# Six kinds of small matmuls with a moving operand of 32 or 64 columns in place of 1 to 32

## The chip, the cores and the metric

The kernel runs on one core of one Trainium2 chip. The metric is the device time of one execution in microseconds, given as the median of several runs.

## The reference

Two layers of a decode step for four tokens (batch B = 4, one query each). A layer is attention over the last 2048 positions of a cache, with a residual, and then a gated feed-forward with a residual. Both layers use the same weights and the same caches.

```python
W = 2048                                  # of 8192 cached positions
q = (layernorm(x) @ wq).reshape(B, 16, 256)            # 16 query heads, 8 kv heads
scores = q . k[:, :, -W:] * 256 ** -0.5                # a kv head serves 2 query heads
o = softmax(scores) . v[:, :, -W:]
x = x + o.reshape(B, 4096) @ wo                        # D = 448
h = layernorm(x)
x = x + (silu(h @ w_gate) * (h @ w_up)) @ w_down       # F = 1792
# ... the same two steps once more
```

## The kernel before

The work is cut into pairs of a token and a kv head: 4 tokens, 2 layers and 8 kv heads make 64 pairs. A written table gathers them into 48 groups of one or two pairs. Each group needs the K and V windows of its pairs, 1 MB each, which SP's queue loads into a pool of 34 buffers of 512 KB. Some of them are kept for the second layer. All engines work through orders that are written out by hand as tables of numbers, one per engine, and a small graph places the semaphore waits between them. A buffer is loaded again only after its last reader is done, so the speed of the engines decides when transfers start.

One group goes through these steps. DVE transposes K in place (L853). PE multiplies K with the query (L886, the scores, tile S). DVE takes the maximum per partition (L902, into `tiny`). PE runs the *spread* (L907 and L910): one matmul writes a mask of large negative numbers, and a second adds the maxima of the partitions that belong to one head, so that DVE can take the maximum over them (L916, `negm`). ACT takes the exponential (L920). PE turns the probabilities (L936, tile Y), ACT copies them to pT (L946), PE sums them (L954), DVE and POOL make the reciprocal (L959, L981). PE multiplies with V (L968). ACT and DVE split the result into even and odd parts (L984, L986, `oh`), PE *flips* it back into columns (L992), DVE scales it into oT (L1026), and PE applies wo, as rows (L1046) or as columns (L1038).

The last group goes without the flip. It multiplies V as the weights with the probabilities as the moving operand (L1006, `vs`), which gives columns at once.

At the end of a token's attention the rows are collected: ACT and DVE write them as a high and a low part (L771, L773), PE *turns* them into columns (L781), and DVE adds the residual (L785). The norm follows (L544 to L570), and the feed-forward, with tokens as columns (L730 gate and up, L758 *down*, L766 the residual) or as rows (L666, L694). The feed-forward of the last token has a version of its own (L1152 to L1217) behind the last projection (L1074, L1083).

Some matmuls repeat their moving operand already: in `ffn` a helper named `more` reads the columns of n tokens over and over until 32 are filled, and only the first n of the result are used. PE's order also holds filler matmuls (L1313) with weights of zero and 512 columns, which add nothing to the tile that they name.

The names of the tiles in the profile are those of the first tensor of a kind: `wide` holds the rows and the feed-forward's middle, `tiny` small constants (among them the maxima, `osel` and `rsel`), `small` small numbers in fp32, `half` the pool of buffers.

Of the kernel before, what the change touches and what calls it, by code (L numbers as in the profile page):

```python
# [351 lines left out]
def build(nc, A_x, A_k_cache, A_v_cache, A_wq, A_wo, B_x, B_w_gate, B_w_up, B_w_down, out):  # L352
# [3 lines left out]
    with ExitStack() as es:  # L356
# [342 lines left out]
        def ffn(ts):  # L699
            n, sl = len(ts), span(ts)  # L700
            gw, rep = NFC * n, 32 // n
            cw = n * rep
            th, hc = wide[:, 0:gw], wideb[:, 256:256 + gw]

            def more(ap):
                return ap.unsqueeze(1).broadcast_to([128, rep, n])

            def block(zb, f):
                return zb[:, cw * f:cw * f + cw].rearrange("p (r t) -> p r t", t=n)

            def once(zb, f):
                return zb[:, 0:cw * f].rearrange("p (f x) -> p f x", x=cw)[:, :, 0:n]
            for t in ts:
                s, k = st[:, t, :], f"st{t}"
                g.op(POOL, "fh", lambda e, s=s: e.tensor_single_scalar(s[:, 11:12], s[:, 8:9], 0.5, op=ALU.mult),
                     r=(k + "r2",), w=(k + "s",))
                g.op(POOL, "ft", lambda e, s=s: e.tensor_scalar(s[:, 14:15], s[:, 8:9], s[:, 11:12], None, op0=ALU.mult),
                     r=(k + "r2", k + "s"), w=(k + "t",))

            def gu(e, gi, c0, c1):  # L720
                last = None
                w = (wg_sb, wu_sb)[gi]
                for cc in range(c0, c1):
                    for fc in range(NFC):
                        if cc < 3:
                            lhsT, rhs = w[:, cc * FF + fc * 128:cc * FF + fc * 128 + 128], xn[:, cc, sl]
                        else:
                            lhsT = w[:, 3 * FF + (fc % 7) * 128:3 * FF + (fc % 7) * 128 + 128]
                            rhs = xe[:, fc // 7, sl]
                        last = e.matmul(block((Zb, Z2)[gi], fc), lhsT=lhsT, rhs=more(rhs),  # L730
                                        start=(fc == 0 and cc == 0), stop=(cc == 3), skip_group_check=True)
                return last
            rn, rx = tuple(f"xn{t}" for t in ts), tuple(f"xe{t}" for t in ts)
            for gi, (z, bank, w) in enumerate((("z", "Z", "wg"), ("z2", "Z2", "wu"))):
                g.op(PE, "guc3", lambda e, gi=gi: gu(e, gi, 0, 3), r=rn + (w + "a",), w=(z,), bank=(bank,))
                g.op(PE, "guc1", lambda e, gi=gi: gu(e, gi, 3, 4), r=rx + (w + "b",), acc=(z,), bank=(bank,))

            def tok(ap, j):
                return ap.rearrange("p (f t) -> p t f", t=n)[:, j, :]
            for j, t in enumerate(ts):  # L740
                g.op(SCA, "tanhc", lambda e, j=j, t=t: e.activation(
                    tok(th, j), once(Zb, NFC)[:, :, j], ACT.Tanh, scale=st[:, t, 11:12]),
                    r=("z", f"st{t}s"), w=("wa",), bank=("Z",))
            vec("fca", lambda e: e.scalar_tensor_tensor(
                out=th.rearrange("p (f t) -> p f t", t=n), in0=th.rearrange("p (f t) -> p f t", t=n), scalar=1.0,
                in1=once(Zb, NFC), op0=ALU.add, op1=ALU.mult), ("z",), ("wa",), ("Z",))
            for j, t in enumerate(ts):
                vec("fcb", lambda e, j=j, t=t: e.scalar_tensor_tensor(
                    out=tok(hc, j), in0=tok(th, j), scalar=st[:, t, 14:15],
                    in1=once(Z2, NFC)[:, :, j], op0=ALU.mult, op1=ALU.mult),  # L750
                    ("wa", "z2", f"st{t}t"), ("wa", "wb"), ("Z2",))

            def down(e):
                k, last = 0, None
                for cc in range(4):
                    c0 = 128 * cc if cc < 3 else D - 128
                    for fc in range(NFC):
                        last = e.matmul(block(Zb, cc), lhsT=wd_sb[:, fc, c0:c0 + 128],  # L758
                                        rhs=more(hc[:, n * fc:n * fc + n]), start=(k == 0), stop=(k == 4 * NFC - 1),
                                        skip_group_check=True)  # L760
                        k += 1
                return last
            g.op(PE, "downc", down, r=WIDE + ("wd",), w=("z",), bank=("Z",))
            for j, t in enumerate(ts):
                for x, key in ((xr, f"x{t}"), (xs, f"xs{t}")):
                    vec("fx", lambda e, j=j, t=t, x=x: e.tensor_tensor(  # L766
                        x[:, t, :], x[:, t, :], once(Zb, 4)[:, :, j],
                        op=ALU.add), ("z", key), (key,), ("Z",))

        def rows(t):  # L770
            g.op(SCA, "rowcp", lambda e: e.activation(wideb[:, 0:D], Ab[:, 0:D], ACT.Copy), r=(f"row{t}",), w=("wa",),  # L771
                 bank=("A",))
            vec("rowsub", lambda e: e.tensor_tensor(wideb[:, 512:512 + D], Ab[:, 0:D], wideb[:, 0:D], op=ALU.subtract),  # L773
                (f"row{t}", "wa"), ("wb",), ("A",))

            def turn(e):
                last = None
                for i in range(2):
                    for cc in range(4):
                        c0 = 512 * i + (128 * cc if cc < 3 else D - 128)  # L780
                        last = e.matmul(Zb[:, cc:cc + 1], lhsT=wideb[:, c0:c0 + 128], rhs=rsel[:, t:t + 1],  # L781
                                        start=(i == 0 and cc == 0), stop=(i == 1), skip_group_check=True)
                return last
            g.op(PE, "rturn", turn, r=WIDE + ("rsel",), w=("z",), bank=("Z",))
            vec("rowadd", lambda e: e.tensor_tensor(xr[:, t, :], xs[:, t, :], Zb[:, 0:4], op=ALU.add), ("z", f"xs{t}"),  # L785
                (f"x{t}",), ("Z",))

        def residual(t):
# [37 lines left out]
        def group(gi, members, outs, split, last=False):  # L826
# [77 lines left out]
                r=(f"s{s_}",), w=(f"pmax{s_}",), bank=(f"S{s_}",))  # L904

            def spread(e):
                e.matmul(Sb[s_][0:R, 256:288], lhsT=identb[0:R, 0:R],  # L907
                         rhs=far[0:R, :, :, :].broadcast_to([R, 2, 8, 2]) if w_ == 2 else
                         far1[0:R, :, :].broadcast_to([R, 16, 2]), start=True, stop=False, skip_group_check=True)
                return e.matmul(  # L910
                    Sb[s_][0:R, 256:288].rearrange("p (q x) -> p q x", x=8),
                    lhsT=pmax[s_][0:R, 0:1].broadcast_to([R, R]),
                    rhs=identb[0:R, :].rearrange("p (q x) -> p q x", q=4)[:, :, 0:8], start=False, stop=True,
                    skip_group_check=True)
            g.op(PE, "spread", spread, r=(f"pmax{s_}", "identb", "far", "far1"), w=(f"m{s_}",), bank=(f"S{s_}",))
            g.op(DVE, "negm", lambda e: e.tensor_reduce(  # L916
                negm[s_][0:R, 0:1], Sb[s_][0:R, 256:288], AX.X, ALU.max, negate=True),
                r=(f"m{s_}",), w=(f"negm{s_}",), bank=(f"S{s_}",))
            def ex(e):
                return e.activation(  # L920
# [68 lines left out]

            def flip(e):  # L990
                for dh in range(2):
                    last = e.matmul(Yb[p_][:, 2 * n * dh:2 * n * dh + 2 * n],  # L992
                                    lhsT=oh[:, :].rearrange("p (m e) -> p e m", e=2)[:, dh, :],
                                    rhs=osel[:, 0:2 * n], start=dh == 0, stop=dh == 1, skip_group_check=True)
                return last
            if not last:
                g.op(PE, "flip", flip, r=("oh", "osel"), w=(f"yp{p_}",), bank=(f"Y{p_}",))
# [1 line left out]
            def vs(e, P, hv):  # L999
                x = None  # L1000
                for a in range(2):
                    for gg in range(4):
                        v = unit(vss[P][hv])[:, 1024 * a + 256 * gg:1024 * a + 256 * gg + 256]
                        for dh in range(2):
                            c0 = 32 * (n * dh + P)
                            x = e.matmul(Yb[p_][:, c0:c0 + 32].rearrange("p (r n) -> p r n", n=2),  # L1006
                                         lhsT=v.rearrange("p (m e) -> p e m", e=2)[:, dh, :],
                                         rhs=(pT[pt][:, gg, 2 * a + hv, 8 * P:8 * P + 2] if n == 2 else
                                              p1[:, gg % 2, 2 * a + gg // 2, hv, 0, :]).unsqueeze(1).broadcast_to(
                                                  [128, 16, 2]),  # L1010
                                         start=P == hv == a == gg == dh == 0, stop=False, skip_group_check=True)
                return x
            for P, (pp, t, layer, kvh) in enumerate(members if last else []):
                for hv in range(2):
# [1 line left out]
                    o = g.op(PE, "vs", lambda e, P=P, hv=hv: vs(e, P, hv), r=(f"pT{pt}", f"v{t}_{kvh}_{hv}"),  # L1016
                             bank=(f"Y{p_}",), **kw)
                    o.rel = (vss[P][hv],)
            yo = Yb[p_][:, 0:4 * n].rearrange("p (d P n) -> p d P n", d=2, n=2)
            if last:  # L1020
                yo = Yb[p_][:, 0:64 * n].rearrange("p (d P x) -> p d P x", d=2, P=n)[:, :, :, 0:2]
            for oi, Ps, ts in outs:
                o_ = oT[oi]
                src = yo[:, :, Ps[0]:Ps[-1] + 1, :]
# [355 lines left out]
```

## Time and profile before

| | |
|---|---|
| median of 3 runs | 288.78 us |
| lowest and highest | 287.57 and 292.31 us |
| the profiled execution | 289.3 us |
| its span, from the first to the last instruction | 287.4 us |
| mean granted clock of TensorE, as a share of full speed | 0.958 |
| PE busy | 226.3 us (79% of the span) |
| DVE busy | 190.1 us (66%) |
| ACT busy | 60.8 us (21%) |
| POOL busy | 82.0 us (29%) |
| moved by DMA | 105.66 MB, mean 368 GB/s |

PE is the matmuls, PEld the loads of weights that go on beside them, DVE, ACT and POOL the other engines, SP the engine whose queue issues the loads. In a row by shape, `Z<-wide,wd_sb 128*128 128x32 bf16 x112` names the output, the inputs, the rows and columns of weights in use, the moving operand as partitions times columns, and how many there were. Matmuls overlap, so the time of one in such a row is longer than its distance from the next.

### The profile page before, as it was taken

Reading aid. Unit: us, or ns where it says so; the run is one execution under the profiler, and the core shown is the slowest. Engines: PE = TensorE matmul, PEld = TensorE weight load, DVE = VectorE, ACT = ScalarE, POOL = GpSimd, SP = SyncE. Lnnn points to the kernel's source line nnn. Section 1 sums busy time; section 2 is a strip of 40 time slices with the busy share of each in tenths; the row PEclk is TensorE's granted clock in tenths of the full one; section 3 lists DMA queues with packets and bytes.
Section 4 is the critical chain, followed back from the end, with each engine's and each line's share of the span. In section 5 each row is a group of like instructions: output and inputs, shape, how many; then the busy total and the mean of one; then the engine's idle time right before and its main releaser. Section 6 shows DMA issues by size and latency. Waiting matters only on the chain.

```text
span 287.4 us, 10703 instructions
## 1 busy us (share of the span) xinstructions
PE 226.3 (79%) x4710; PEld 129.9 (45%) x4710; DVE 190.1 (66%) x586; ACT 60.8 (21%) x173; POOL 82.0 (29%) x228
## 2 busy tenths in 40 slices
PE   5011679978888698697987989989987599988686
PEld 1000224454474444354444654454554347655476
DVE  2598738945512578976954898768689559758532
ACT  2000011312301221122232112222432131224210
POOL 1000241323022313222432142630542325243241
PEclk9999999989999989999999999989999959999959
DMA  7999999999996999999999999999999998799900
GB/s 288 412 419 417 419 411 407 396 404 407 393 380 190 349 414 415 417 405 408 351 388 403 424 415 409 414 412 409 413 413 408 406 368 299 212 386 412 392 16 4
DMA packets 26311, 105.66 MB, mean 368 GB/s; under 512 B 2580, under 2 KB 6680, under 8 KB 21528
## 3 DMA queue, kind: packets, MB, share of 16 engines
q1 hardware_dynamic: 26256, 104.97, 92.5%
q8 instruction: 37, 0.61, 0.8%
q14 instruction: 10, 0.08, 0.1%
q10 hardware_dynamic: 8, 0.00, 0.0%
HBM read 104.96 MB, written 0.00 MB: 365 GB/s over the span
## 4 chain that ended last, share of the span: by engine, by line
PE 45%; DMA 24%; DVE 20%; issue 5%; ACT 3%; SPq 2%; POOL 1%; DVEq 0%; ACTq 0%
DMA half<-in_A_v_cache_dram 15%; DVE half L853 10%; PE S L886 10%; PE Y L968 6%; DMA half<-in_A_k_cache_dram 5%; DMA wo_sb<-in_A_wo_dram 4%; PE Z L1313 4%; PE A L1046 3%; PE Z L730 2%; PE S L1313 2%; PE Y L936 2%; PE Z L604 2%; DVE oh L986 2%; PE Z L550 2%; PE Z L666 2%
## 5 line engine op out<-in xcount | busy, mean ns | idle before, releaser
L853 DVE STREAM_TRANSPOSE half<-half 128x1024 uint32<-128x1024 uint32 x86 | 104.3, 1228 | 6.6 <-DMA half<-in_A_k_cache_dram 6.6
L981 POOL TENSOR_TENSOR small<-small 128x2 f32<-128x2 f32 (+1 forms) x48 | 38.4, 805 | 50.9 <-DVE small L959 46.2
L968 PE MATMUL Y<-half,pT 128*4 128x256 bf16 (+1 forms) x992 | 45.2, 279 | 7.2 <-issue 3.6
L886 PE MATMUL S<-half,qe 128*8 128x128 bf16 (+1 forms) x1536 | 44.9, 244 | 6.4 <-issue 2.4
L886 PEld LDWEIGHTS S<-half,qe 128*8 128x8 bf16 x1536 | 30.2, 86 | 19.3 <-issue 5.2
L1313 PE MATMUL Z<-identb,small 128*128 128x512 bf16 x111 | 36.8, 388 | 0.4 <-DVE wide L627 0.4
L920 ACT ACTIVATE praw<-S,small 104x128 bf16<-104x128 f32 (+1 forms) x48 | 19.3, 401 | 53.0 <-DVE small L916 45.8
L892 POOL TENSOR_TENSOR qe<-qc,tiny 128x64 bf16<-128x64 bf16 x64 | 17.8, 292 | 39.7 <-PE S L886 27.1
L986 DVE SCALAR_TENSOR_TENSOR oh<-oh,small,Y 128x256 bf16<-128x256 bf16 x47 | 22.1, 470 | 8.9 <-ACT oh L984 8.4
L968 PEld LDWEIGHTS Y<-half,pT 128*4 128x4 bf16 (+1 forms) x992 | 19.0, 84 | 18.6 <-issue 6.4
L984 ACT ACTIVATE oh<-Y 128x256 bf16<-128x256 f32 x47 | 18.0, 382 | 44.2 <-PE Y L968 31.6
L902 DVE TENSOR_REDUCE tiny<-S 104x1 bf16<-104x128 f32 (+1 forms) x48 | 15.7, 329 | 10.2 <-PE S L886 9.8
L566 POOL TENSOR_SCALAR st<-st 128x1 f32<-128x1 f32 x15 | 4.0, 264 | 58.0 <-DVE st L556 57.8
L946 ACT ACTIVATE pT<-Y 128x64 bf16<-128x64 f32 (+1 forms) x48 | 12.2, 257 | 36.9 <-PE Y L936 29.4
L1046 PE MATMUL A<-wo_sb,oT 128*4 128x448 bf16 x204 | 17.8, 384 | 1.3 <-DVE oT L1026 1.2
L1313 PE MATMUL A<-identb,small 128*128 128x512 bf16 x38 | 15.8, 496 | 2.9 <-DVE A L444 2.7
L1247 POOL MEMSET oT<- 128x16 bf16 x37 | 4.0, 111 | 45.6 <-PE A L1046 31.9
L610 ACT ACTIVATE wide<-Z,small 128x512 bf16<-128x512 f32 x10 | 6.4, 684 | 48.2 <-PE Z L604 38.5
L550 PE MATMUL Z<-st,small 128*128 128x2 f32 x30 | 6.6, 290 | 12.6 <-DVE selt L461 9.3
L1026 DVE TENSOR_TENSOR oT<-Y,small 128x4 bf16<-128x4 f32 (+1 forms) x63 | 9.0, 156 | 10.4 <-PE Y L992 7.0
L959 DVE TENSOR_REDUCE small<-Y 128x2 f32<-128x32 f32 (+1 forms) x48 | 9.1, 190 | 9.3 <-PE Y L954 8.9
L916 DVE TENSOR_REDUCE small<-S 104x1 f32<-104x32 f32 x48 | 8.4, 176 | 8.0 <-PE S L910 7.7
(188 smaller groups left out, 302.0 us busy)
## 6 DMA issues: line engine op xcount, KB each, us to landing
half<-in_A_v_cache_dram SPq DMA_DIRECT2D x91, 512.0 KB, 9.8
half<-in_A_k_cache_dram SPq DMA_DIRECT2D x34, 1024.0 KB, 9.7
half<-in_A_k_cache_dram SPq DMA_DIRECT2D x18, 512.0 KB, 8.0
wo_sb<-in_A_wo_dram SPq DMA_DIRECT2D x8, 448.0 KB, 11.5
half<-in_A_wq_dram SPq DMA_DIRECT2D x3, 1024.0 KB, 16.3
wd_sb<-in_B_w_down_dram SPq DMA_DIRECT2D x1, 1568.0 KB, 16.7
wg_sb<-in_B_w_gate_dram SPq DMA_DIRECT2D x1, 1344.0 KB, 10.1
wu_sb<-in_B_w_up_dram SPq DMA_DIRECT2D x1, 1344.0 KB, 13.1
```

What stands on the lines that cost most here:

```text
L550: g.op(PE, "nstat", lambda e: e.matmul(Z2[:, 0:2], lhsT=onesf[:, 0:1].broadcast_to([128, 128]), rhs=s[:, 0:2], start=True, stop=True, skip ...
L853: return e.transpose(a, a)
L886: last = e.matmul(Sb[s_][qd:qd + 8, 0:32 * 2 * J], lhsT=qe[q_][:, P, ce, :, :].rearrange("p a n -> p (a n)"), rhs=keys(kcs[P], J * x, J, c ...
L892: g.op(POOL, "qe", lambda e, P=P, t=t, kvh=kvh: e.tensor_tensor(qe[q_][:, P, :, :, :], qc[t][:, kvh, :, :].unsqueeze(2).broadcast_to([128, ...
L902: g.op(DVE, f"max{w_}", lambda e: e.tensor_reduce(pmax[s_][0:R, :], Sb[s_][0:R, 0:N], AX.X, ALU.max), r=(f"s{s_}",), w=(f"pmax{s_}",), ban ...
L920: return e.activation(praw[0:R, 0:N].rearrange("p (g r l) -> p g r l", g=2 * w_, l=2), Sb[s_][0:R, 0:N].rearrange("p (l g r) -> p g r l", ...
L968: last = e.matmul(Yb[p_][32 * gg:32 * gg + M, 256:512], lhsT=pT[pt][:, gg, 2 * a + hv, 4 * P:4 * P + M] if n == 2 else p3[:, gg, 2 * a + h ...
L981: g.op(POOL, f"pow{n}", lambda e: e.tensor_tensor(ri[p_][:, 0:2 * n], rs[p_][:, 0:2 * n], expo[:, 1:1 + 2 * n], op=ALU.pow), r=(f"rs{p_}", ...
L984: g.op(SCA, "oh", lambda e: e.activation(oh[:, :], Yb[p_][:, 256:512], ACT.Copy), r=(f"y{p_}",), w=("oh",), bank=(f"Y{p_}",))
L986: g.op(DVE, "oho", lambda e: e.scalar_tensor_tensor(out=oh[:, :], in0=oh[:, :], scalar=lomask[:, 0:1], in1=Yb[p_][:, 256:512], op0=ALU.mul ...
L1046: last = e.matmul(Ab[32 * k:32 * k + B, 0:D], lhsT=oT[oi][:, k % 2, k // 2, :], rhs=wo_sb[:, 4 * kvh + k, :], start=False, stop=False, ski ...
L1313: return e.matmul(fill_banks[b][:, 0:512], lhsT=zero[:, 0:1].broadcast_to([128, 128]), rhs=identb[:, :].unsqueeze(1).broadcast_to([128, 4, ...
```

## The change

Six kinds of matmuls read their moving operand repeatedly, until it has 32 or 64 columns, and write as many columns of the output. The later reader takes the first copy only, out of columns that lie further apart.

| matmul | lines | count | columns before | columns now |
|---|---|---|---|---|
| down projection, tokens as columns | L758 | 112 | 32 | 64 |
| turn of the rows | L781 | 88 | 1 | 32 |
| spread, the mask | L907 | 48 | 32 | 64 |
| spread, the maxima | L910 | 48 | 32 | 64 |
| flip | L992 | 94 | 2 or 4 | 64 |
| V times probabilities in the last group | L1006 | 64 | 32 | 64 |

The readers are L766, L785, L916 and L1026. On every engine the same instructions stand in the same order as before; PE's differ in these widths only, and the waits, the buffers and the fillers stay.

```diff
             def down(e):
-                        last = e.matmul(block(Zb, cc), lhsT=wd_sb[:, fc, c0:c0 + 128],
-                                        rhs=more(hc[:, n * fc:n * fc + n]), ...
+                        last = e.matmul(Zb[:, 64 * cc:64 * cc + 64].rearrange("p (r t) -> p r t", t=n),
+                                        lhsT=wd_sb[:, fc, c0:c0 + 128],
+                                        rhs=hc[:, n * fc:n * fc + n].unsqueeze(1).broadcast_to([128, 64 // n, n]), ...
             vec("fx", ...
-                        x[:, t, :], x[:, t, :], once(Zb, 4)[:, :, j],
+                        x[:, t, :], x[:, t, :], Zb[:, 0:256].rearrange("p (f x) -> p f x", x=64)[:, :, j],
...
             def turn(e):
-                        last = e.matmul(Zb[:, cc:cc + 1], lhsT=wideb[:, c0:c0 + 128], rhs=rsel[:, t:t + 1],
+                        last = e.matmul(Zb[:, 32 * cc:32 * cc + 32], lhsT=wideb[:, c0:c0 + 128],
+                                        rhs=rsel[:, t:t + 1].broadcast_to([128, 32]),
...
             def spread(e):
-                e.matmul(Sb[s_][0:R, 256:288], lhsT=identb[0:R, 0:R],
-                         rhs=far[0:R, :, :, :].broadcast_to([R, 2, 8, 2]) if w_ == 2 else
-                         far1[0:R, :, :].broadcast_to([R, 16, 2]), ...
+                e.matmul(Sb[s_][0:R, 256:320], lhsT=identb[0:R, 0:R],
+                         rhs=far[0:R, :, :, :].broadcast_to([R, 2, 16, 2]) if w_ == 2 else
+                         far1[0:R, :, :].broadcast_to([R, 32, 2]), ...
                 return e.matmul(
-                    Sb[s_][0:R, 256:288].rearrange("p (q x) -> p q x", x=8),
+                    Sb[s_][0:R, 256:320].rearrange("p (q r x) -> p q r x", r=2, x=8),
                     lhsT=pmax[s_][0:R, 0:1].broadcast_to([R, R]),
-                    rhs=identb[0:R, :].rearrange("p (q x) -> p q x", q=4)[:, :, 0:8], ...
+                    rhs=identb[0:R, :].rearrange("p (q x) -> p q x", q=4)[:, :, 0:8].unsqueeze(2).broadcast_to([R, 4, 2, 8]), ...
             g.op(DVE, "negm", lambda e: e.tensor_reduce(
-                negm[s_][0:R, 0:1], Sb[s_][0:R, 256:288], AX.X, ALU.max, negate=True),
+                negm[s_][0:R, 0:1], Sb[s_][0:R, 256:320].rearrange("p (q r x) -> p q r x", r=2, x=8)[:, :, 0, :], AX.XY, ALU.max, negate=True),
...
             def flip(e):
-                    last = e.matmul(Yb[p_][:, 2 * n * dh:2 * n * dh + 2 * n],
+                    last = e.matmul(Yb[p_][:, 64 * dh:64 * dh + 64].rearrange("p (r x) -> p r x", x=2 * n),
                                     lhsT=oh[:, :].rearrange("p (m e) -> p e m", e=2)[:, dh, :],
-                                    rhs=osel[:, 0:2 * n], ...
+                                    rhs=osel[:, 0:2 * n].unsqueeze(1).broadcast_to([128, 32 // n, 2 * n]),
...
             def vs(e, P, hv):
-                            c0 = 32 * (n * dh + P)
-                            x = e.matmul(Yb[p_][:, c0:c0 + 32].rearrange("p (r n) -> p r n", n=2),
+                            c0 = 64 * (n * dh + P)
+                            x = e.matmul(Yb[p_][:, c0:c0 + 64].rearrange("p (r n) -> p r n", n=2),
-                                                  [128, 16, 2]),
+                                                  [128, 32, 2]),
```

More of the change, by code (lines that the diff above doesn't have):

```diff
@@ L757, in down @@
                     for fc in range(NFC):
-                        last = e.matmul(block(Zb, cc), lhsT=wd_sb[:, fc, c0:c0 + 128],
-                                        rhs=more(hc[:, n * fc:n * fc + n]), start=(k == 0), stop=(k == 4 * NFC - 1),
+                        last = e.matmul(Zb[:, 64 * cc:64 * cc + 64].rearrange("p (r t) -> p r t", t=n),
+                                        lhsT=wd_sb[:, fc, c0:c0 + 128],
+                                        rhs=hc[:, n * fc:n * fc + n].unsqueeze(1).broadcast_to([128, 64 // n, n]), start=(k == 0), stop=(k == 4 * NFC - 1),
                                         skip_group_check=True)
@@ L784, in rows @@
             g.op(PE, "rturn", turn, r=WIDE + ("rsel",), w=("z",), bank=("Z",))
-            vec("rowadd", lambda e: e.tensor_tensor(xr[:, t, :], xs[:, t, :], Zb[:, 0:4], op=ALU.add), ("z", f"xs{t}"),
+            vec("rowadd", lambda e: e.tensor_tensor(
+                xr[:, t, :], xs[:, t, :], Zb[:, 0:128].rearrange("p (c x) -> p c x", x=32)[:, :, 0], op=ALU.add), ("z", f"xs{t}"),
                 (f"x{t}",), ("Z",))
@@ L906, in spread @@
             def spread(e):
-                e.matmul(Sb[s_][0:R, 256:288], lhsT=identb[0:R, 0:R],
-                         rhs=far[0:R, :, :, :].broadcast_to([R, 2, 8, 2]) if w_ == 2 else
-                         far1[0:R, :, :].broadcast_to([R, 16, 2]), start=True, stop=False, skip_group_check=True)
+                e.matmul(Sb[s_][0:R, 256:320], lhsT=identb[0:R, 0:R],
+                         rhs=far[0:R, :, :, :].broadcast_to([R, 2, 16, 2]) if w_ == 2 else
+                         far1[0:R, :, :].broadcast_to([R, 32, 2]), start=True, stop=False, skip_group_check=True)
                 return e.matmul(
-                    Sb[s_][0:R, 256:288].rearrange("p (q x) -> p q x", x=8),
+                    Sb[s_][0:R, 256:320].rearrange("p (q r x) -> p q r x", r=2, x=8),
                     lhsT=pmax[s_][0:R, 0:1].broadcast_to([R, R]),
-                    rhs=identb[0:R, :].rearrange("p (q x) -> p q x", q=4)[:, :, 0:8], start=False, stop=True,
+                    rhs=identb[0:R, :].rearrange("p (q x) -> p q x", q=4)[:, :, 0:8].unsqueeze(2).broadcast_to([R, 4, 2, 8]), start=False, stop=True,
                     skip_group_check=True)
@@ L991, in flip @@
                 for dh in range(2):
-                    last = e.matmul(Yb[p_][:, 2 * n * dh:2 * n * dh + 2 * n],
+                    last = e.matmul(Yb[p_][:, 64 * dh:64 * dh + 64].rearrange("p (r x) -> p r x", x=2 * n),
                                     lhsT=oh[:, :].rearrange("p (m e) -> p e m", e=2)[:, dh, :],
-                                    rhs=osel[:, 0:2 * n], start=dh == 0, stop=dh == 1, skip_group_check=True)
+                                    rhs=osel[:, 0:2 * n].unsqueeze(1).broadcast_to([128, 32 // n, 2 * n]),
+                                    start=dh == 0, stop=dh == 1, skip_group_check=True)
                 return last
@@ L1018, in group @@
                     o.rel = (vss[P][hv],)
-            yo = Yb[p_][:, 0:4 * n].rearrange("p (d P n) -> p d P n", d=2, n=2)
+            yo = Yb[p_][:, 0:128].rearrange("p (d x) -> p d x", d=2)[:, :, 0:2 * n].rearrange("p d (P n) -> p d P n", n=2)
             if last:
-                yo = Yb[p_][:, 0:64 * n].rearrange("p (d P x) -> p d P x", d=2, P=n)[:, :, :, 0:2]
+                yo = Yb[p_][:, 0:128 * n].rearrange("p (d P x) -> p d P x", d=2, P=n)[:, :, :, 0:2]
             for oi, Ps, ts in outs:
```

## The prediction

> **What bounds the kernel now.** I read the page first, for the share of each engine and of the DMA, then the windows view for the granted clock, then the chain of waits for the tail.
>
> ```profile
> span 287.4 us, 10703 instructions
> PE 226.3 (79%) x4710; PEld 129.9 (45%) x4710; DVE 190.1 (66%) x586; ACT 60.8 (21%) x173; POOL 82.0 (29%) x228
> PEclk9999999989999989999999999989999959999959
> GB/s 288 412 419 417 419 411 407 396 404 407 393 380 190 349 414 415 417 405 408 351 388 403 424 415 409 414 412 409 413 413 408 406 368 299 212 386 412 392 16 4
> ```
>
> The bandwidth row sits near 410 GB/s for most of the span. There the transfers are the limit, and an engine that gains or loses a few tenths of a microsecond only moves its own slack. The row drops in three places: around 84 to 98 us, around 236 to 252 us, and in the last two slices, the tail, where nothing is left to load. In those places the chain through PE, DVE and POOL is the limit. In the PEclk row the lowest digits stand at the second drop and at the tail. The windows view, cut where the clock changes, shows them sharply. Its columns are the stretch, the busy time of PE, weight load, DVE, ACT and POOL, the granted clock, the DMA share and GB/s.
>
> ```profile
> 188.40:191.81 3.41, 3.10 (x78) 2.14 (x70) 1.84 (x13) 0.45 (x2) 0.48 (x2) 1.00 1.00 407
> 191.81:195.23 3.42, 3.17 (x38) 1.23 (x33) 2.77 (x6) 1.04 (x2) 2.15 (x9) 0.50 1.01 410
> 225.95:229.36 3.41, 1.51 (x48) 0.89 (x46) 1.64 (x5) 0.50 (x2) 1.68 (x4) 1.00 1.03 406
> 229.36:232.77 3.41, 3.01 (x37) 1.18 (x38) 1.03 (x5) 1.12 (x4) 0.71 (x1) 0.50 1.03 414
> 232.77:236.19 3.42, 3.42 (x38) 1.35 (x39) 1.89 (x8) 1.42 (x4) 0.91 (x3) 0.50 0.94 378
> 236.19:239.60 3.41, 3.41 (x95) 2.25 (x93) 3.17 (x11) 0.00 (x0) 0.00 (x0) 1.00 0.55 207
> 270.32:273.73 3.41, 1.65 (x49) 1.20 (x37) 1.91 (x12) 0.86 (x3) 1.15 (x3) 1.00 0.78 309
> 273.73:277.14 3.41, 3.25 (x72) 2.45 (x73) 1.27 (x5) 0.87 (x2) 1.01 (x1) 0.50 0.02 7
> 277.14:280.56 3.42, 3.42 (x102) 3.01 (x99) 1.36 (x13) 0.00 (x0) 2.16 (x8) 0.50 0.03 7
> 280.56:283.97 3.41, 3.41 (x110) 3.22 (x108) 1.09 (x7) 0.44 (x2) 0.72 (x1) 1.00 0.02 5
> ```
>
> The clock is either 1.00 or 0.50, and it changes on a grid of 3.41 us. Each step seems to answer to the stretch before it. The stretch from 188.40 had PE busy for 3.10 of 3.41 us and was still followed by 0.50, so busy time is not what counts. I therefore counted moving columns, with four matmuls that fill different quarters of the array as one. Here is the stretch 229.36 to 232.77 grouped by shape (busy us and mean ns of one behind the bar):
>
> ```profile
> L968 PE MATMUL Y<-half,pT 128*4 128x256 bf16 x16 | 1.2, 396 | 0.0
> L1313 PE MATMUL Z<-identb,small 128*128 128x512 bf16 x2 | 1.2, 588 | 0.0
> L1046 PE MATMUL A<-wo_sb,oT 128*4 128x448 bf16 x4 | 0.6, 577 | 0.0
> L968 PE MATMUL Y<-half,pT 128*8 128x256 bf16 x5 | 0.6, 385 | 1.9 <-issue 1.9
> L936 PE MATMUL Y<-sel,praw 104*64 104x32 bf16 x4 | 0.3, 224 | 0.0
> L907 PE MATMUL S<-small,identb 104*104 104x32 bf16 x1 | 0.3, 266 | 0.0
> L910 PE MATMUL S<-identb,tiny 104*104 104x32 bf16 x1 | 0.2, 249 | 0.0
> L992 PE MATMUL Y<-tiny,oh 128*128 128x2 bf16 x2 | 0.2, 188 | 0.0
> L992 PE MATMUL Y<-tiny,oh 128*128 128x4 bf16 x2 | 0.2, 176 | 0.0
> ```
>
> That is 1024 + 1024 + 448 + 320 + 64 + 32 + 32 + 4 + 8 = 2956 columns, and the clock stayed at 0.50. The two stretches with 1.51 and 1.65 us of PE work were far thinner and shut the gate. My estimate from these is that about 3000 columns in a stretch hold the gate open, or open it.
>
> **The change part by part.** No instruction is added, removed or moved; only widths change. So the cost is in longer matmuls, and any gain has to come through the clock. The rate of one column comes from the same sixteen matmuls of 256 columns at both clocks (start, us, what), four at a time and so 1024 columns deep; under them stand the L758 run of 56 and a projection of the tail, and then, from the table by shape (mean ns of one before the second bar), a matmul of 64 columns and three kinds that change:
>
> ```profile
> 234.51 1.02 PE L968 MATMUL Y<-half,pT 128*4 128x256 bf16 x16
> 236.67 0.61 PE L968 MATMUL Y<-half,pT 128*4 128x256 bf16 x16
> 246.81 1.56 PE L758 MATMUL Z<-wide,wd_sb 128*128 128x32 bf16 x56
> 274.06 0.92 PE L1046 MATMUL A<-wo_sb,oT 128*4 128x448 bf16 x8
> L1207 PE MATMUL Y<-identb,wide 128*4 128x64 bf16 x2 | 0.2, 192 | 0.0
> L907 PE MATMUL S<-small,identb 104*104 104x32 bf16 x48 | 9.6, 207 | 1.7 <-DVE tiny L902 1.7
> L992 PE MATMUL Y<-tiny,oh 128*128 128x2 bf16 x64 | 6.3, 168 | 2.0 <-DVE oh L986 1.8
> L781 PE MATMUL Z<-tiny,wide 128*128 128x1 bf16 x88 | 3.8, 164 | 0.2 <-DVE wide L773 0.2
> ```
>
> The difference, 0.41 us over 1024 columns, is 0.40 ns a column; if half the clock doubles the cost of a column, a column costs 0.40 ns open and 0.80 ns shut, with 0.2 us fixed.
>
> *Down projection (L758, 112 matmuls, 32 to 64 columns).* It runs at 1.56 / 56 = 28 ns a matmul, and 64 columns at 0.40 ns are 26 ns. With the clock open, weight loading and issue cover the extra columns: nothing. Without that cover it is 112 x 13 ns = 1.4 us. The Trainium skill, in "TensorE: Matmul & The Clock Gate", section "Back-to-back issue gap", states that 1 to 64 columns all cost about 60 cycles, 25 ns; by that the cost is nothing too, but the same section gives N / 1.2 ns at the cold clock, 53 ns for 64 columns, and that speaks against the change in the tail.
>
> *Flip (L992), spread (L907 and L910), row turn (L781).* These are single links between DVE steps. Going from 168 to the 192 ns of a 64-column matmul is 24 ns, and the second flip adds some 6 ns of spacing: 30 ns a flip. A spread goes up by 32 columns in the link that DVE waits for, 13 ns, with a little spacing: 20 ns. A turn also gains about 20 ns. The reads of the result take the same number of elements, only further apart, so I cost them at nothing (0 to 10 ns each). How many lie on a path shows in the waits (waiter, releaser: us in total, times, longest):
>
> ```profile
> DVE small L916 <- PE S L910: 7.7, 10, 2.5
> DVE oT L1026 <- PE Y L992: 7.0, 10, 2.4
> ```
>
> Ten spreads and ten flips ended a wait of DVE: 10 x 20 + 10 x 30 ns = 0.5 us; the turns are too few to matter. The bounds are 0, if DMA waits absorb them all, and 2.6 us if all 48 spreads, 47 flips and 11 turns count. I take +0.5.
>
> *The last group (L1006, 64 matmuls, 32 to 64 columns).* The chain at the tail:
>
> ```profile
> 275.55 0.95 PE Y L1006 x32
> 276.50 0.28 PE Z L781 x8
> 276.78 0.88 PE Y L1006 x32
> 277.69 0.43 PE S L1280 x2
> 278.57 0.85 PE S L1083 x32
> 279.42 0.43 PE S L1313
> 281.32 0.54 PE Z L1152 x21
> ```
>
> Both halves run at 0.50. At 0.80 ns a column, 64 columns take 51 ns against 28 to 30, so the first half goes from 0.95 to 1.65 us: +0.7. The stretch from 273.73 then carries more. From 275.55 to 277.14 it streams up to 1.59 us / 0.80 ns = 2000 columns, where 32-column matmuls at 28 to 30 ns, with the turn between, gave some 1500, and 8 x 448 / 4 = 896 of L1046 come on top: 2900 against 2400. That is close to the line, and I take it that the gate opens at 277.14. Then the second half costs what it does now (28 ns), and the work behind it up to 280.56 speeds up: L1280 and L1313 by 0.2 us each, as 512 columns at 0.40 ns less show for the latter, and the 48 + 40 thin matmuls from about 28 to the 26 ns of L1152 at 281.32, some 0.2. Together -0.6. The tail comes out at +0.1, with the bounds -0.6 and, if the gate stays shut, +1.5.
>
> *The middle.* In the stretch from 229.36 the widened matmuls add 2 x 32 + 2 x 62 + 2 x 60 = 308 columns to 2956: 3264. By my estimate that opens the clock at 232.77 instead of 236.19. The stretch from 232.77 has PE busy for 3.42 of 3.42 us and about as many columns, 3000 x 0.40 ns = 1.2 us less; behind it the DMA falls to 207 GB/s while PE is full, so an earlier PE there frees buffers earlier and shortens the drop. I take -1.0; the bounds are 0 and -1.4. The stretch from 191.81 also ran at 0.50, but at 410 GB/s, and I count nothing for such.
>
> **Sum.** The profiled execution took 289.3 us, 0.5 above the median of 288.78. 289.3 + 0.5 (links) + 0.1 (tail) + 0.0 (down) - 1.0 (middle) = 288.9, and the same against the median gives **288.4 us**: no difference that can be told. About 2% (below 283.0, above 294.6) is what a measurement of this kernel can tell from no change, since its three runs span 287.57 to 292.31.
>
> **The rivals.**
>
> *Slower: the gate does not open for the columns, and the tail pays.* Both halves of L1006 then run at 51 ns a matmul on a chain that nothing covers: 64 x 23 ns = +1.5 us, with the links 288.8 + 1.5 + 0.5 = 290.8. For it: I have a handful of stretches, not a law, and the count ahead of 277.14 is close to the line. It decides if the clock still reads 0.50 after the first half of the last group. The Trainium skill, "TensorE: Matmul & The Clock Gate", section "HAM oscillation — how this bites in real kernels", lays the drop to idle gaps of PE of more than about 3.4 us; by that rule wider matmuls do nothing to the clock, and 290.8 is the time. The trace speaks against it in the row from 188.40, where 3.10 us of busy PE was followed by 0.50.
>
> *The middle is hidden anyway.* The clock opens at 232.77, but the buffers that the next transfers wait for come free by DVE's transposes (DVE was busy 3.17 of 3.41 us from 236.19) and not by PE: 288.8 + 0.5 + 0.1 = 289.4. Against it: PE was the fuller engine, 3.41 of 3.41.
>
> *Clearly faster.* All four shut stretches from 229.36 on open, 4 x 1.2 = 4.8 us less, against 0.5 of links and some 0.7 of spacing: 285.2. Against it: the stretches from 225.95 and 270.32 are half empty because PE stood still (the 1.9 us before L968 are "issue"), and a few hundred columns do not fill them.
>
> **How the numbers follow.** The forecast has 0.4, the unopened gate 0.25, the hidden middle 0.2, the fast case 0.15. Which stretches are shut depends on where the 3.41 us grid falls in an execution, so each case spreads by about 1.2 us, one stretch's worth. The range that leaves out 2 in 10 is 285.2 to 291.5. Only the outer ends of the fast case pass 283.0, and only all links at 2.6 us with the shut tail and a bad grid pass 294.6: faster 0.06, same 0.89, slower 0.05.
>
> **What would show it.** In the changed profile L758 should stay at 26 to 30 ns a matmul, L992 should read about 192 ns and L910 about 213. Fewer stretches at 0.50 would bear out the column count, above all one instead of two at the tail. I am wrong on the mechanism if the number of 0.50 stretches is the same with the same columns around them, and on the size if the 236 us drop stays as deep while they vanish.

## The result and the profile after

| | before | after |
|---|---|---|
| median of 22 executions | 289.81 us | 290.95 us |
| mean of the same | 289.88 us | 290.99 us |
| the profiled execution, its span | 289.3, 287.4 us | 289.98, 288.1 us |

The ratio after to before is 1.0083, with a 95% interval of 1.0055 to 1.011. That ratio leaves out executions more than 1.5% above the fastest of their kernel; one very fast execution of the kernel before (285.57 us) makes it leave out 10 of the 22 of before and 2 of the 22 of after, so I also give the difference of the means over all executions, with 1.96 standard errors: **+1.1 us, give or take 0.9**. A second comparison, in other rounds (e16, below), gave +1.9 ± 1.3; both together, weighted by their errors, +1.4 ± 0.75 us. So the change makes the kernel slower by about half a per cent. The forecast was 288.4 us, 0.4 us below the median of then: a small loss came in place of no change.

The page of the kernel after:

```profile
span 288.1 us, 10703 instructions
PE 227.6 (79%) x4710; PEld 131.9 (46%) x4710; DVE 190.6 (66%) x586; ACT 60.7 (21%) x173; POOL 82.1 (28%) x228
PEclk9655569999999899799999999999999979999959
GB/s 287 412 418 419 419 411 406 396 401 408 394 380 190 362 407 419 412 408 406 320 350 397 419 416 409 414 420 402 412 413 411 406 389 334 253 366 411 361 13 3
```

The shape is that of before: the same three drops of bandwidth. The 5s near the start are no news: the 24 matmuls of L604 that start at 37.2 us took 2.73 us in both profiles, with the clock given as 1.00 before and as 0.50 here. The record of the clock begins at 41.6 us in the profile of before and at 6.7 us in this one, and the row shows full clock up to there. So the mean of 0.958 given for the kernel before counts 41.6 us that were not recorded.

The middle and the tail of the kernel after, in the windows view (stretch, busy time of PE, weight load, DVE, ACT, POOL, granted clock, DMA share, GB/s):

```profile
228.52:231.93 3.41, 1.89 (x36) 0.87 (x24) 1.14 (x6) 0.68 (x4) 1.86 (x4) 1.00 1.01 400
231.93:235.34 3.41, 3.41 (x47) 1.46 (x47) 1.31 (x6) 1.63 (x6) 1.33 (x4) 0.50 1.04 420
235.34:238.76 3.42, 3.16 (x79) 2.11 (x72) 3.30 (x8) 0.46 (x2) 0.00 (x0) 1.00 0.80 304
269.48:272.89 3.41, 2.28 (x61) 1.70 (x61) 2.11 (x13) 0.86 (x3) 1.21 (x3) 1.00 0.93 366
272.89:276.30 3.41, 3.25 (x45) 2.46 (x46) 0.99 (x3) 0.87 (x2) 1.01 (x1) 0.50 0.14 50
276.30:279.72 3.42, 3.42 (x86) 3.42 (x83) 0.80 (x7) 0.00 (x0) 1.74 (x6) 0.50 0.00 0
```

In the middle one stretch is at 0.50 where there were two. At the tail there are still two. The time went into two places. The first is the down projection. The kernel before's run for a single token, which the prediction did not show (start, us, what, and the idle time before it):

```profile
85.45 1.90 PE L758 MATMUL Z<-wide,wd_sb 128*128 128x32 bf16 x56 [0.19 <-DVE wide L748]
```

and both runs of the kernel after:

```profile
83.89 3.40 PE L758 MATMUL Z<-wide,wd_sb 128*128 128x64 bf16 x56 [0.19 <-DVE wide L748]
...
247.14 1.87 PE L758 MATMUL Z<-wide,wd_sb 128*128 128x64 bf16 x56
```

The first grew by 1.50 us, the second by 0.31. The waits say who paid, in the kernel before and in the kernel after:

```profile
DVE xr L766 <- PE Z L758: 2.0, 1, 2.0
```

```profile
DVE xr L767 <- PE Z L758: 3.9, 2, 3.5
```

The second place is the last group, in the chain of waits after:

```profile
274.71 1.81 PE Y L1010 x32
276.52 0.21 PE Z L782 x8
276.73 1.71 PE Y L1010 x32
```

From the start of the first half to the end of the second it takes 3.73 us, where 2.11 stood before.

### The profile page after: what moved, and what is told of

It reads as the page before. It is cut to its first block, busy times and chain, and to the rows that moved or that the text cites. A ratio compares the mean times of both kernels' runs of the same rounds, so it can differ in the third digit from the quotient of the medians.

```text
span 288.1 us, 10703 instructions
## 1 busy us (share of the span) xinstructions
PE 227.6 (79%) x4710; PEld 131.9 (46%) x4710; DVE 190.6 (66%) x586; ACT 60.7 (21%) x173; POOL 82.1 (28%) x228
## 4 chain that ended last, share of the span: by engine, by line
PE 42%; DMA 25%; DVE 22%; issue 4%; ACT 3%; SPq 2%; POOL 1%; DVEq 0%; ACTq 0%
DMA half<-in_A_v_cache_dram 16%; DVE half L856 12%; PE S L889 8%; DMA half<-in_A_k_cache_dram 6%; PE Y L971 5%; PE Z L1317 4%; DMA wo_sb<-in_A_wo_dram 4%; PE A L1050 3%; PE Z L730 2%; DVE oh L989 2%; PE Y L939 2%; PE Z L604 2%; PE Z L758 2%; PE Z L550 2%; PE A L1317 2%
## 5 line engine op out<-in xcount | busy, mean ns | idle before, releaser
L971 PE MATMUL Y<-half,pT 128*4 128x256 bf16 (+1 forms) x992 | 43.5, 274 | 7.7 <-DMA half<-in_A_v_cache_dram 4.1
L889 PE MATMUL S<-half,qe 128*8 128x128 bf16 (+1 forms) x1536 | 43.8, 243 | 5.2 <-DVE half L856 1.8
L889 PEld LDWEIGHTS S<-half,qe 128*8 128x8 bf16 x1536 | 29.4, 85 | 17.8 <-DVE half L856 4.1
L971 PEld LDWEIGHTS Y<-half,pT 128*4 128x4 bf16 (+1 forms) x992 | 18.3, 83 | 20.1 <-DMA half<-in_A_v_cache_dram 6.4
L1317 PEld LDWEIGHTS Z<-identb,small 128*128 128x128 bf16 x111 | 9.5, 100 | 9.4 <-issue 5.5
L995 PE MATMUL Y<-tiny,oh 128*128 128x64 bf16 x94 | 10.9, 198 | 3.6 <-DVE oh L989 3.4
```

The source lines that it names most:

```text
L889: last = e.matmul(Sb[s_][qd:qd + 8, 0:32 * 2 * J], lhsT=qe[q_][:, P, ce, :, :].rearrange("p a n -> p (a n)"), rhs=keys(kcs[P], J * x, J, c ...
L971: last = e.matmul(Yb[p_][32 * gg:32 * gg + M, 256:512], lhsT=pT[pt][:, gg, 2 * a + hv, 4 * P:4 * P + M] if n == 2 else p3[:, gg, 2 * a + h ...
L1317: return e.matmul(fill_banks[b][:, 0:512], lhsT=zero[:, 0:1].broadcast_to([128, 128]), rhs=identb[:, :].unsqueeze(1).broadcast_to([128, 4, ...
```

## The experiments

Every line gives the ratio with its 95% interval and then, from the mean over all executions, the difference to the kernel before in us with 1.96 standard errors. The standard errors take executions as independent. e15 shows why both are needed.

**e1_down32.** The change with the down projection back.

```diff
-    Zb[:, 64 * cc:64 * cc + 64] ... rhs=hc[...].unsqueeze(1).broadcast_to([128, 64 // n, n])
+    block(Zb, cc) ... rhs=more(hc[:, n * fc:n * fc + n])
```

> The change with the down projection (L758) back at 32 columns; the other five kinds stay wide. Theory A (the piece theory: a moving operand that is read in many separate pieces costs about 1 ns a piece, so that 64 pieces of one column take 60 ns and not 26): the first run of 56 goes back from 3.40 to about 1.90 us and the second from 1.87 to 1.56, both in stretches where PE sets the pace, and 1.6 of the change's 2.4 us go: a ratio to the kernel before of about 1.003. Rival B (the wide matmuls at the tail, at the low clock, and the links carry the loss, the down projection is covered as predicted): the ratio stays at about 1.008.

1.0035 (1.0000 to 1.0071); +1.7 ± 1.1 us. The runs were back at 1.90 and 1.56 us. The ratio fits theory A. The means over all executions do not show the gain: +1.7 is no less than the +1.1 of the whole change. That is taken up again in e17.

**e2_down_only.** The kernel before with `down` and its reader as in the change.

> The kernel before with the down projection alone at 64 columns. Theory A: first run of 56 at 3.4 us, second at 1.87 us, 1.5 to 1.8 us more in all: a ratio of 1.005 to 1.006. Rival B: the loss is elsewhere, ratio 1.000, and the longer run at 84 us is swallowed by the stretch behind it.

1.0063 (1.0026 to 1.0100); +1.5 ± 1.0 us. The runs took 3.39 and 1.87 us, as in the change, 1.8 us more in all, and the end moved by 1.5. For theory A.

**e3_last_only.** The kernel before with the last group as in the change.

> The kernel before with the last group's matmuls (L1006) alone at 64 columns. Where the clock is low in that stretch, each half should take 1.7 to 1.8 us in place of 0.9, and as nothing covers the tail the whole gets 1.5 to 1.7 us longer: ratio 1.004 to 1.006 if the tail's clock stays low in most executions (Theory A needs this for the rest of the loss, Rival B for most of it). If the wider matmuls open the clock one step earlier, as predicted, only the first half pays and the ratio is 1.000 to 1.002.

1.0049 (1.0002 to 1.0096); +0.8 ± 1.1 us. The chain at its tail:

```profile
272.05 1.89 PE Y L1006 x32
273.94 0.19 PE Z L781 x8
274.13 1.46 PE Y L1006 x32
```

Here the clock did open within the second half (at 275.1), and the two halves still took 3.54 us from start to end, 1.4 more than before. The place pays. Over all executions the end of the kernel is not clear of the noise; what the profiles of all runs show of it stands under "The last group" below.

**e4_down_flat.** The change, with another way of writing the single column.

```diff
-    rhs=hc[:, fc:fc + 1].unsqueeze(1).broadcast_to([128, 64, 1])
+    rhs=hc[:, fc:fc + 1].broadcast_to([128, 64])        # one token only
```

> The whole change, but for a single token the down projection reads its one column as a flat pattern of 64 (one piece of 64 repeats) in place of 64 pieces of one. The columns, the weights and the tile are the same. Theory A: the first run of 56 falls from 3.40 to 1.6 us (28 ns a matmul) and the ratio from 1.008 to about 1.003. Rival B', that a repeated single column is slow however it is written (the same 2 bytes are fetched 64 times): it stays at 3.4 us and 1.008.

1.0036 (0.9998 to 1.0074); +2.0 ± 1.2 us. The run of the single token:

```profile
86.57 1.90 PE L759 MATMUL Z<-wide,wd_sb 128*128 128x64 bf16 x56 [0.19 <-DVE wide L748]
```

The same 64 columns, weights and tile: 1.90 in place of 3.40 us. So not the repetition is slow but the pieces. It is 31 ns a matmul, (1.90 - 0.2) / 55, and not the 28 expected: 64 columns are not free either. The source writes the output of a single token flat as well, but in the built program the output is one run of 64 columns in both kernels, so only the reading differs. The kernel as a whole did not get faster by it: +2.0 ± 1.2 us, against +1.1 ± 0.9 for the change.

**e5_links_only.** The kernel before with flip, spread and row turn as in the change.

> The kernel before with the flip, the two spread matmuls and the row turn alone widened; the down projection and the last group stay at 32. By the prediction's links: ten to twelve of each on a path, +0.5 us, a ratio of 1.002. By the sum of the runs so far (down alone 1.006, last group alone 1.005, the whole change 1.008) the links come to -0.002 to +0.001, nothing that can be told. If the rest of the loss hides in the links, 1.004 or more.

0.9955 (0.9913 to 0.9997); -1.2 ± 1.0 us. No loss in the links, if anything a gain.

**e6_flat32.** No width changed; in `ffn`, for one token:

```diff
-    ap.unsqueeze(1).broadcast_to([128, 32, 1])
+    ap.broadcast_to([128, 32])
```

> The kernel before, with gate, up and down for a single token reading their one column as a flat pattern of 32 in place of 32 pieces of one; all widths stay. Theory A (about 1 ns a piece): the runs of 42 at 80 to 84 us fall from 1.48 us (35 ns a matmul) to about 1.2 (28 ns, as with two tokens), the down run from 1.90 to 1.56, about 1.1 us less on a path that PE sets: ratio 0.996. If 34 ns is the pace of loading weights in that stretch whatever the pattern, nothing changes: 1.000.

0.9966 (0.9929 to 1.0002); -0.8 ± 0.9 us. The gate's run of 42, in the kernel before:

```profile
79.89 1.48 PE L730 MATMUL Z<-xn,wg_sb 128*128 128x32 bf16 x42 [0.40 <-DVE xn L554]
```

and with the flat pattern:

```profile
77.83 1.22 PE L731 MATMUL Z<-xn,wg_sb 128*128 128x32 bf16 x42 [0.40 <-DVE xn L554]
```

1.48 to 1.22 us, 25 ns a matmul in place of 31. The kernel before paid for its pieces already. The down projection of the single token missed its expectation:

```profile
82.71 0.29 PE L759 MATMUL Z<-wide,wd_sb 128*128 128x32 bf16 x5 [0.18 <-DVE wide L749]
83.34 1.43 PE L759 MATMUL Z<-wide,wd_sb 128*128 128x32 bf16 x51 [0.34 <-issue]
```

Its matmuls ran at 25 ns too, but PE stood still for 0.34 us behind the fifth, for no reason that the profile shows. From start to end the run took 2.06 us, where 1.56 was expected and 1.90 stood before.

**e7_links_256.** The links alone, with flip and spread at 256 columns.

> The links alone, but with flip and spread at 256 columns (row turn at 32), to magnify their price. A flip gets about 0.2 us longer than before and a spread 0.18 (222 to 252 columns of 0.4 ns twice). If only the ten to twelve of each that ended a wait of DVE count: 12 x 0.2 + 11 x 0.18 = 4.4 us, a ratio of 1.015. If nearly all of them lie on the path: 18 us, 1.06. If DMA waits absorb them: below 1.005.

1.0064 (1.0027 to 1.0101); +1.7 ± 0.9 us, far below 4.4. The digits of its clock:

```profile
PEclk9999999999979999999999999997999999999999
```

Between 42 and 286 us the mean clock was 0.99, against 0.95 in the profile of before and 0.97 in that of after. The fuller stretches kept the clock up, but the links at 256 cost more than that brings. PE was also busy for longer, 218.7 us of those 244 in place of 211.1 before, so this run alone does not part columns from busy time.

**e8_down128** and **e9_down128_flat.** The kernel before with 128 columns in the down projection; in e9 the single token reads them flat.

> The kernel before with the down projection at 128 columns, in pieces: 128 of one column for one token, 64 of two for two tokens. Theory A: the first run of 56 takes about 121 ns a matmul, 6.8 us, and the second about 64 ns, 3.6 us; together +7 us on a path that PE sets, ratio 1.02 or more. By columns alone (0.4 ns each): 51 ns a matmul, 2.9 us in both runs, +2.3 us, ratio 1.008.

> The run before with 128 columns in the down projection, but for a single token read as a flat pattern (two tokens keep 64 pieces of two). If a piece of one column costs about 0.9 ns (two columns' time) and a flat column 0.42 ns: the first run falls from 6.38 us to 56 x 56 ns + 0.2 = 3.3 us, the second stays at 3.36 us, and the ratio falls from 1.022 to about 1.012. If repeating one column is slow in itself: 6.4 us again and 1.022.

e8: 1.0225 (1.0169 to 1.0281), +6.7 ± 1.4 us. e9: 1.0061 (1.0017 to 1.0106), +2.1 ± 1.2 us. The single token's run in e8:

```profile
85.36 6.38 PE L758 MATMUL Z<-wide,wd_sb 128*128 128x128 bf16 x56 [0.19 <-DVE wide L748]
```

and both runs in e9:

```profile
84.64 3.39 PE L759 MATMUL Z<-wide,wd_sb 128*128 128x128 bf16 x56 [0.19 <-DVE wide L748]
...
247.21 3.36 PE L759 MATMUL Z<-wide,wd_sb 128*128 128x128 bf16 x56
```

Flat, and in 64 pieces of two, 128 columns take 57 to 58 ns a matmul, 0.45 ns a column; 128 pieces of one take 112. So a piece of one column costs about as much as two columns. And the loss reaches the end: in e8 the two runs grew by 4.48 and 1.80 us (3.36 against 1.56), 6.3 in all, and the kernel by 6.7 ± 1.4 (four executions).

**e10_links_flat.** e5 and e6 together.

> The two parts that gained, together: links wide (flip, spread, row turn), and gate, up and down at 32 columns with a flat pattern for a single token; the last group stays at 32. If both gains are real and lie at different places: 0.9955 x 0.9966 = 0.992, some 2.3 us below the kernel before. If the links' 0.9955 was chance: 0.996 to 0.997.

0.9906 (0.9863 to 0.9949); -1.7 ± 1.4 us, median 287.72 against 289.25 us. The largest gain of the study: wide links, flat patterns, and down projection and last group left at 32 columns. It is not told apart from that of the links alone, -1.2 ± 1.0.

**e11_flip_only** and **e12_spread_turn.** The links in two parts.

> The kernel before with the flip alone at 64 columns. By the link prices of the prediction: ten to twelve on a path, 30 ns each, +0.35 us, ratio 1.001. If wide links gain through the clock, the flip carries most of it, since it adds 94 x 62 = 5800 of the links' 11600 columns: 0.997 to 0.998.

> The kernel before with the spread at 64 and the row turn at 32 columns; the flip stays narrow. By the link prices: +0.2 us, ratio 1.001. If the links' 0.9955 is real and adds up, this and the flip alone multiply to about 0.9955; if it was chance, both lie within 0.003 of 1 and their product too.

e11: 0.9957 (0.9910 to 1.0004), but +0.5 ± 1.5 us over all executions. e12: 0.9945 (0.9903 to 0.9987), -0.6 ± 1.2 us. Each has a part of the links. Their sum is 0.0 ± 2.0, and weighted with e5, which has all of them, -0.9 ± 0.9 us. A loss of half a microsecond is not there; a gain is at the edge of the errors and not shown.

**e13_flip_twice**, **e14_fill64**, **e15_before_again.** The delay without the columns, the columns without the links, and nothing.

```diff
-    for dh in range(2):            # flip, e13
+    for dh in (0, 0, 1):
...
+    e.matmul(fill_banks[b][:, 0:64], lhsT=<zeros>, rhs=identb[:, 0:64], ...)   # ahead of each filler, e14
```

> The kernel before with the first of the flip's two matmuls run twice (2 or 4 columns each, the second run overwrites the first with the same values). It makes every flip later by some 25 ns, as the 64 columns do, but adds hardly a column. If wide links gain through the clock, that is by columns, this gains nothing: 1.000 to 1.002. If they gain because a small delay happens to suit the fixed orders and the transfers, this gains like them: 0.995 to 0.997.

> The kernel before with a further matmul of zeros, 64 columns, ahead of each of the 184 fillers: 11800 columns, as many as the wide links add, at other places, and 184 x 27 ns = 5 us more PE time, in part where PE is idle. If columns as such gain through the clock: below 1.000. If the fillers stand where the stretches are thick already, or if the links gained by something else: 1.003 to 1.010 for the PE time.

> The kernel before, unchanged, measured as a change. Any theory expects 1.000; its distance from 1 shows what such a comparison gives for nothing, against which the links' 0.9955 has to be held.

e13: 1.0050 (1.0015 to 1.0085), -1.2 ± 1.6 us. e14: 1.0118 (1.0020 to 1.0216), +2.1 ± 2.2 us. e15: 1.0081 (1.0030 to 1.0132), 0.0 ± 1.5 us. The kernel before against itself, by the ratio, came out as far from 1 as the change had; in those rounds the executions of before ran from 284.21 to 294.98 us. By the means it is where it must be. e13 and e14 tell nothing apart: the two measures of e13 have opposite signs.

**e16_change**, **e17_change_down32**, **e18_change_last32.** The whole change, without its down projection, and without its last group, on one chip.

> The whole change, this time on the same chip and in the same rounds as its two parts undone (the two runs below). From the parts measured alone, over all executions: down +1.5 us, last group +0.8, links -1.2, together +1.1 us above the kernel before.

> The whole change with the down projection back at 32 columns. If the loss in the down projection reaches the end (its runs are 1.5 and 0.3 us shorter here, in stretches that PE sets): 1.5 us less than the whole change of these rounds. If what follows absorbs it, as the first such run suggested: the same as the whole change.

> The whole change with the last group back at 32 columns. The two halves at the tail get 1.5 us shorter with nothing behind them to absorb it: 1.0 to 1.6 us less than the whole change of these rounds. If wide matmuls there open the clock for what follows, as predicted, the difference is below 0.3 us.

e16: 1.0100 (1.0051 to 1.0149), +1.9 ± 1.3 us. e17: 1.0081 (1.0034 to 1.0128), +1.1 ± 1.2 us. e18: 1.0108 (1.0035 to 1.0180), +1.8 ± 1.6 us. e17 is below e16, but by 0.8 ± 1.2 us, which is inside the errors. In e18 the tail was as in the kernel before:

```profile
276.55 0.95 PE Y L1010 x32
277.51 0.29 PE Z L782 x8
277.80 0.85 PE Y L1010 x32
```

That is 2.10 us from start to end, so the tail itself gained what was expected, and yet the whole did not show it. Parts of 1 to 1.5 us are at the edge of what six or twelve executions with a standard deviation of about 1.5 to 3 us can tell.

## Why the prediction was wrong, point by point

The forecast was 0.4 us less, and the kernel took 1.1 ± 0.9 us more. Two terms of the sum failed, the down projection at 0.0 and the tail at +0.1; the links, at +0.5, were too high.

**Down projection: this step failed.** "With the clock open, weight loading and issue cover the extra columns: nothing." The runs cost +1.5 and +0.3 us with the clock at 1.00. I took the pace from the run at 246.81 (28 ns) and did not read the other, at 85.45, where the same 56 matmuls of the same width took 1.90 us. Its 34 ns had no cover left: 32 pieces of one column were already the limit, and doubling them doubled the time. e4, e6, e8 and e9 show the cause, e2 and e8 that it reaches the end of the kernel before. With the down projection undone in the whole change (e1, e4, e17) no gain is clear of the noise, so how much of the change's own loss it makes is open. The bound I gave for the uncovered case, 1.4 us, came near to the 1.8 us by luck, and I gave it no weight: it spreads 13 ns over all 112 matmuls, where one run of 56 paid 27 ns each and the other 6.

**The last group: mis-sized.** The rise per matmul when the clock is shut was right (1.81 / 32 = 57 ns where 51 was forecast). That the gate would open at 277.14 and pay the second half back was wrong in this profile: both stretches stayed at 0.50, and the term was +1.6 us where I took +0.1 and gave +1.5 as the bound. Even where the clock opened in time for part of the second half (e3) the halves took 1.4 us more. Over all executions the noise hides it: e3 says +0.8 ± 1.1, and e18 against e16 shows nothing (-0.1 ± 1.6 us). But no other work follows the tail, and in the profiles it stands apart. This is the time from the start of the last group's first half to the end of the span:

| columns in the last group | profiles | time |
|---|---|---|
| 32 | 14 | 11.5 to 12.1 us, mean 11.8 |
| 64 | 6 (after, e1, e3, e4, e16, e17) | 12.7 to 13.5 us, mean 13.1 |

So the term was +1.2 us on average where I took +0.1. The shut stretches do not make the difference: five of the six profiles with 64 columns had one at the tail, as had eight of the fourteen with 32. One of these is e15, the unchanged kernel, whose other profile, the one that I costed, had two. The 0.6 us that an opened gate was to pay back stood on that one execution.

**The links: not borne out.** The single matmuls grew as forecast, from 168 to 198 ns for the flip and to 212 for the second spread, in the kernel after (mean ns of one ahead of the second bar):

```profile
L995 PE MATMUL Y<-tiny,oh 128*128 128x64 bf16 x94 | 10.9, 198 | 3.6 <-DVE oh L989 3.4
L913 PE MATMUL S<-identb,tiny 104*104 104x64 bf16 x48 | 9.8, 212 | 0.0
```

The readers, costed at nothing, took what they took before (medians of 180 and 181 ns for `negm`, 157 and 158 ns into oT). But the kernels with links alone give -0.9 ± 0.9 us where +0.5 was forecast. Counting the waits that such a matmul ends was too much. The reason is argued and not shown: ending a wait of DVE need not put a matmul on the path that sets the end. Whether the links gain through the clock stays open.

**The middle.** One shut stretch in place of two came as forecast in the profile after, and for the reason forecast: the stretch from 231.93 had 3297 columns (3264 were forecast) and opened the clock, where 2956 had not. But it is one execution, and the grid falls elsewhere in each. In the profiles that I have, kernels with narrow links and with links at 64 columns do not differ in a way that I could call shown; only e7 stands apart, with two shut stretches behind 42 us where the other nineteen profiles have 3 to 10. The -1.0 us is neither confirmed nor refuted.

**The column count** was an estimate from a handful of stretches. Counted in the same way over all twenty profiles, with each matmul in the stretch in which it starts, it holds:

| columns in a stretch | stretches | next one at 1.00 |
|---|---|---|
| below 2500 | 144 | 3 |
| 2500 to 3250 | 184 | 123 |
| 3250 and more | 1186 | 1183 |

So there is a band and not a line. Busy time parts them worse: 26 stretches in which PE was busy for 3.0 us or more were followed by 0.50, and 24 of these had fewer than 3250 columns. At the tail the count was off for the kernel before: the stretch from 273.73 had 2628 columns and not 2400. Its counterpart after, from 272.89, had 3036, inside the band, and the clock stayed at 0.50.

**The slower rival** named the tail as its place and 290.8 us as its time, near to the 290.95 measured. That is partly luck: it adds 2.0 us to a median of 288.78, which further executions put at 289.81, and 0.5 of the 2.0 stand for the links, where no loss showed. Half of its reason was right: the tail pays. The loss in the down projection was in none of the rivals.

**The Trainium skill**, "TensorE: Matmul & The Clock Gate", section "Back-to-back issue gap", has 1 to 64 columns at about 25 ns. The runs here agree at 32 columns in pairs or flat (25 ns) and not at 64, where the same weights and tile took 31 ns flat and 58 ns in single columns. Its N / 1.2 ns for the low clock, 53 ns at 64 columns, agrees with the 53 to 57 ns of the last group's halves.

## What to carry to other kernels

Before a matmul is costed by its columns, read each of its runs apart: two runs of one line with different times (1.90 and 1.56 us here) say that something other than the width sets the pace, and the change may multiply just that. When one column is to be repeated, write it as one flat run of repeats and not as many pieces of one. Measure the kernel against itself before an effect of half a per cent is explained. And where the spread of executions hides a part of 1 us, time the stretch that it lies in over all profiles, as with the tail here.

## What the runs showed of the hardware

At 64 and 128 columns a moving operand in pieces of a single column ran at half the pace of a flat or paired one; at 32 columns it took 31 ns against 25. With the clock at 1.00, run time less 0.2 us, over the number of matmuls less one (55, and 41 in the run of 42):

| columns | single pieces | pairs | flat |
|---|---|---|---|
| 32 | 31 ns (1.90 us) | 25 ns (1.56 us) | 25 ns (42 matmuls in 1.22 us) |
| 64 | 58 ns (3.40 us) | 30 ns (1.87 us) | 31 ns (1.90 us) |
| 128 | 112 ns (6.38 us) | 57 ns (3.36 us) | 58 ns (3.39 us) |

Between 64 and 128 columns that is 0.84 ns a single piece and 0.42 ns a column otherwise. The 25 ns at 32 columns are more than 32 x 0.42 = 13 ns, so there the columns do not set the pace; what does is not shown.
